# Splitting float64 weights: the high part read before the low word is added, the sum kept in the rounded word's two buffers

## The chip, the core and the metric

The kernel runs on one core of one Trainium2 chip, as one launch. The metric is the device time of an execution in microseconds (us); a run is one such time, and a kernel is told by the median of its runs.

## The reference

Attention over 4 batches, 12 heads, 448 tokens and a head size of 64, with an RMS norm and a gain on queries and keys, and then two mixers over tokens and channels on the result (4 x 448 x 768):

```python
q_n, k_n = rmsnorm(q, g_q), rmsnorm(k, g_k)
x = softmax(q_n @ k_n.T / 8) @ v            # joined heads: 4 x 448 x 768
# mixer 1: rank 32 over tokens, 768 -> 3072 -> 768 over channels
u = x + (xt @ U @ V).transpose(0, 2, 1);     x = u + np.maximum(u @ wa1, 0) @ wa2
# mixer 2: 448 -> 256 -> 448 over tokens, 768 -> 1536 -> 768 over channels
u = x + (np.maximum(xt @ wt1, 0) @ wt2).transpose(0, 2, 1)
x = u + np.maximum(u @ wb1, 0) @ wb2
```

Here xt is x with tokens and channels exchanged. The weights (U, V, wa1, wa2, wt1, wt2, wb1, wb2) arrive as float64, so the kernel reads each as two 32-bit words.

## The kernel before

TensorE multiplies in fp32r. To keep float32 accuracy, most operands are split into a high part (rounded to fp32r) and a low part (what is left of it), and a product is three matmuls: high by high, low by high, high by low (`three`, and the loops in `first` and `second`, line 79 in the profile).

A weight is made from float64 in chunks of up to 128 x 768. For each of them `to_f32` loads the words (L116, tile `w_raw`, two buffers) and then issues: ScalarE takes the absolute value of the high word (L125, into `w_bits`, two buffers); VectorE clamps it (L126), shifts and masks it (L127) and puts sign and top exponent bit back (L131); ScalarE rounds the low word to an integer (L130, into `w_round`, one buffer); GpSimd adds the two (L134, into `w_bits`). `split` then lets ScalarE round the sum to the high part (L144) and GpSimd subtract to get the low part (L145), both into slots `wh` and `wl` of four buffers each, which are free again when TensorE has used a chunk. `load_w` also stores the sum (L159, queue SP, tensors `c_a`, `c_b`) for the chunks that a later stage wants whole, and the split parts (L170, `h_a`, `h_b`). 80 chunks are made in all, 72 of them of 128 x 768.

The work runs in stages. Up to about 195 us there is attention for batches 0 and 1 alone. Then `rank_mix` of these two, and the first channel mixer (`ffn("a", ...)`) for them, with attention for batches 2 and 3 laid between its steps by `run` up to about 610 us; then the rest of that mixer, the token mix, and the second mixer's `ffn("b", ...)`. All weights are made in this part, up to about 940 us. After that `pair_ffn` does the same for batches 2 and 3 with weights from the stores. In `ffn` a group is two chunks of the first weight and two of the second; `first` gives four products per group, and `relu` splits each (ScalarE L628, then VectorE L629, tile `gs`) before `second` can use them.

A scheduler puts the instructions of each engine in order from their dependencies; each engine then works in that order and waits at the first instruction that isn't ready. DMAs are nearly all issued from SP, also in order. VectorE also computes the maxima of the softmax (L445), the low parts of probabilities (L488, tile `pl`), and the sums onto the residual (L659); ScalarE the exponentials (L447) and copies of transposed probabilities (L484); GpSimd the scaling of the softmax (L450, L454), parts of the norm, and the low part of the mixed activations in the rank and token mix (L556).

## Time and profile before

| | before |
|---|---|
| median of 3 runs | 1542.95 us (1540.15 to 1544.28) |
| the profiled execution's own time | 1534.37 us |
| its span, first to last instruction | 1532.5 us |
| mean granted TensorE clock | 0.981 |
| TensorE matmul busy | 1440.4 us |
| VectorE, GpSimd, ScalarE busy | 1173.5, 933.7, 744.9 us |

The profiled execution lies 1.87 us above its span and 8.58 us below the median of the runs shown. A busy engine is one whose instruction runs; the granted clock is the share of its full speed that TensorE was given.

### The profile page before, as it was taken

The numbers are of one execution on the slowest core, as the hardware profiler recorded it, in microseconds if no ns is written. First come the engines' busy times: TensorE is split into PE (matmuls) and PEld (weight loads), VectorE is DVE, ScalarE is ACT, GpSimd is POOL, SyncE is SP. The second block draws the span as 40 slices with busy tenths as digits, with TensorE's granted clock in tenths as the row PEclk, the third lists the DMA queues.
The fourth block names the chain that finished last, engine by engine and source line by source line (L and its number), as shares of the span: only waits on it lengthen the run. The fifth ranks groups of instructions, "written<-read, shape, count | busy, mean of one in ns | idle before, by whom it ended". The sixth has DMA issues, their size and how long they took to land.

```text
span 1532.5 us, 22085 instructions
## 1 busy us (share of the span) xinstructions
PE 1440.4 (94%) x7396; PEld 1275.7 (83%) x7396; DVE 1173.5 (77%) x1785; ACT 744.9 (49%) x1507; POOL 933.7 (61%) x963
## 2 busy tenths in 40 slices
PE   4988978899899999999999999999999999999997
PEld 3766667798788989888888998889999998988996
DVE  6888887887778787666876766487989888577876
ACT  4777755666656656343644343235343431334431
POOL 6888977786776666354665444047787755206841
PEclk9999988999999999999999999999999999999999
DMA  6666655767766665664646664364545463423333
GB/s 167 158 154 154 156 179 185 239 208 213 227 184 214 201 212 192 227 217 162 217 146 206 235 238 155 114 235 129 181 129 180 129 186 125 136 84 122 123 122 103
DMA packets 144385, 266.06 MB, mean 174 GB/s; under 512 B 12832, under 2 KB 104448, under 8 KB 144160
## 3 DMA queue, kind: packets, MB, share of 16 engines
q1 hardware_dynamic: 143952, 264.65, 55.5%
q8 instruction: 59, 0.97, 0.3%
q14 instruction: 54, 0.44, 0.1%
q10 hardware_dynamic: 320, 0.00, 0.0%
HBM read 149.72 MB, written 79.10 MB: 149 GB/s over the span
## 4 chain that ended last, share of the span: by engine, by line
PE 65%; DVE 11%; DMA 8%; POOL 7%; ACT 5%; issue 4%; SPq 1%; ACTq 0%; POOLq 0%; DVEq 0%
PE ps_x L79 26%; PE ps_g L79 13%; PE ps_p L79 10%; PE pv L79 3%; PE sc L79 3%; PE pt L473 3%; PE ps_u L79 2%; DVE w_bits L126 2%; PE ps_t L79 2%; DMA ks<-both 1%; POOL w_bits L134 1%; POOL w L145 1%; DMA w_raw<-in_moe_w_ch_dram 1%; ACT p L447 1%; DMA c_a<-w_bits 1%
## 5 line engine op out<-in xcount | busy, mean ns | idle before, releaser
L79 PE MATMUL ps_x<-gs,w 128*128 128x448 f32 x1440 | 327.5, 374 | 16.4 <-DVE gs L629 11.4
L79 PE MATMUL ps_g<-u,w 128*128 128x448 f32 x1440 | 313.3, 370 | 5.8 <-DVE gs L629 2.9
L79 PEld LDWEIGHTS ps_x<-gs,w 128*128 128x128 f32 x1440 | 270.6, 192 | 42.0 <-DVE gs L629 14.1
L79 PEld LDWEIGHTS ps_g<-u,w 128*128 128x128 f32 x1440 | 269.8, 189 | 30.4 <-DVE gs L629 3.2
L79 PE MATMUL ps_x<-gs,w_b 128*128 128x448 f32 x1026 | 226.8, 366 | 5.3 <-DVE xT L821 3.5
L79 PEld LDWEIGHTS ps_x<-gs,w_b 128*128 128x128 f32 x1026 | 191.9, 188 | 22.9 <-DVE xT L821 5.0
L134 POOL TENSOR_TENSOR w_bits<-w_bits,w_round 128x768 uint32<-128x768 uint32 (+3 forms) x80 | 144.7, 1808 | 92.7 <-DVE w_bits L131 43.5
L145 POOL TENSOR_TENSOR w<-w_bits,w 128x768 fp32r<-128x768 f32 (+3 forms) x82 | 149.5, 1829 | 84.2 <-ACT w L144 75.9
L659 DVE TENSOR_TENSOR xT<-ps_x,xT 128x448 f32<-128x448 f32 x216 | 132.2, 617 | 47.3 <-PE ps_x L79 45.5
L145 POOL TENSOR_TENSOR w_b<-w_f,w_b 128x384 fp32r<-128x384 f32 x104 | 118.8, 1158 | 55.4 <-ACT w_b L144 55.3
L454 POOL TENSOR_SCALAR p<-p,sm 112x448 f32<-112x448 f32 x192 | 132.5, 703 | 25.4 <-DVE sm L451 23.3
L447 ACT ACTIVATE p<-sc,nm 112x448 f32<-112x448 f32 x192 | 121.1, 633 | 55.0 <-DVE nm L445 51.1
L295 POOL TENSOR_TENSOR w_f<-w_f 128x384 f32<-128x384 f32 x26 | 37.2, 1432 | 179.5 <-DVE pu L730 69.9
L79 PE MATMUL sc<-ks,qs 128*112 128x448 f32 x384 | 120.5, 406 | 19.0 <-DMA ks<-both 11.3
L445 DVE TENSOR_REDUCE nm<-sc 112x1 f32<-112x448 f32 x192 | 116.1, 614 | 24.2 <-PE sc L79 23.3
L473 PEld LDWEIGHTS pt<-ident,p 112*112 112x112 f32 x768 | 90.1, 135 | 38.8 <-issue 11.2
L473 PE MATMUL pt<-ident,p 112*112 112x112 f32 x768 | 112.4, 262 | 5.7 <-POOL p L454 4.6
L126 DVE TENSOR_SCALAR w_bits<-w_bits 128x768 f32<-128x768 f32 (+3 forms) x80 | 78.0, 975 | 47.9 <-ACT w_bits L125 47.3
L484 ACT ACTIVATE ph<-pt 112x448 fp32r<-112x448 f32 (+1 forms) x168 | 88.7, 543 | 44.7 <-PE pt L473 43.6
L130 ACT ACTIVATE w_round<-w_raw 128x768 uint32<-128x768 uint32 (+3 forms) x80 | 69.7, 871 | 73.6 <-POOL w_bits L134 70.3
L763 ACT ACTIVATE pu<-pu 128x448 f32<-128x448 f32 x56 | 32.4, 579 | 136.2 <-DVE pu L752 136.1
L125 ACT ACTIVATE w_bits<-w_raw 128x768 f32<-128x768 f32 (+3 forms) x80 | 69.9, 875 | 56.4 <-POOL w L145 36.2
(139 smaller groups left out, 2780.0 us busy)
## 6 DMA issues: line engine op xcount, KB each, us to landing
w_raw<-in_moe_w_ch_dram SPq DMA_DIRECT2D x72, 768.0 KB, 5.1
w_b<-h_a SPq DMA_DIRECT2D x65, 384.0 KB, 4.2
h_a<-w SPq DMA_DIRECT2D x56, 384.0 KB, 3.0
ks<-both SPq DMA_DIRECT2D x92, 224.0 KB, 3.6
c_a<-w_bits SPq DMA_DIRECT2D x40, 384.0 KB, 5.1
w_f<-c_a SPq DMA_DIRECT2D x40, 384.0 KB, 3.2
h_b<-w SPq DMA_DIRECT2D x32, 384.0 KB, 2.7
w_b<-h_b SPq DMA_DIRECT2D x29, 384.0 KB, 4.1
```

The costliest lines, as they stand in the source:

```text
L79: nc.tensor.matmul(o, lhsT=l, rhs=r, start=start, stop=stop)
L125: nc.scalar.activation(f(w), f(high), AF.Abs)
L126: nc.vector.tensor_scalar_max(f(w), f(w), TINY)
L130: nc.scalar.activation(r, low, AF.Copy, scale=2.0 ** -29)
L134: nc.gpsimd.tensor_tensor(w, w, r, op=ALU.add)
L145: nc.gpsimd.tensor_sub(lo, w, f(hi))
L445: nc.vector.tensor_reduce(nm, sc, axis=AX.X, op=ALU.max, negate=True)
L447: nc.scalar.activation(p, sc, AF.Exp, bias=nm, accum_out=sm[:, c % 2:c % 2 + 1])
L454: nc.gpsimd.tensor_scalar(x, x, sm[:, i:i + 1], 1.0, op0=ALU.mult, op1=ALU.mult)
L473: nc.tensor.transpose(pt[:, c * CP:(c + 1) * CP], pr[c][:, kc * CP:(kc + 1) * CP], ident[:CP, :CP],)
L484: nc.scalar.activation(ph, pt, AF.Copy)
L659: nc.vector.tensor_add(xT[:, dc], px, xT[:, dc])
```

## The change

`to_f32` now returns two values. The first, `near`, is `w_bits` after VectorE's last step: it holds sign, exponent and the upper 20 bits of the mantissa. The second is the sum, which GpSimd now writes over the rounded word `w_round`. `split` rounds the high part from `near`, so this instruction depends on VectorE alone, and the low part is still the sum less the high part. The rounded word has two buffers, one in the old place and one in a pool `cv` (chunks take them in turn). The pool takes the place of the unused pool `hs` in the first stages and is opened again with the buffers of the second mixer. `pl` has two buffers instead of three from the end of the first attention on. The store L159 reads the sum from `w_round`. No instruction is added or dropped.

```diff
--- before.py
+++ after.py
@@ -110,6 +110,8 @@
         return pool.tile(shape, F32, tag=pool.name, name=name)
 
 
+    turns = [0]
+
     def to_f32(srcs, p, n):
         raw = wp.tile([P, n], I64, tag="raw", bufs=2, name="w_raw")
         for o, d in srcs(raw):
@@ -119,7 +121,9 @@
         words = raw[:p].bitcast(U32).rearrange("p (n t) -> p n t", t=2)
         low, high = words[:, :, 0], words[:, :, 1]
         w = wp.tile([P, n], U32, tag="w", bufs=2, name="w_bits")[:p]
-        r = wp.tile([P, n], U32, tag="r", name="w_round")[:p]
+        pool, tag = (wp, "r") if turns[0] % 2 else (pools["cv"], "r2")
+        turns[0] += 1
+        r = pool.tile([P, n], U32, tag=tag, bufs=1, name="w_round")[:p]
 
 
         nc.scalar.activation(f(w), f(high), AF.Abs)
@@ -131,8 +135,8 @@
         nc.vector.scalar_tensor_tensor(
             w, high, 0xC0000000, w, op0=ALU.bitwise_and, op1=ALU.bitwise_or
         )
-        nc.gpsimd.tensor_tensor(w, w, r, op=ALU.add)
-        return f(w)
+        nc.gpsimd.tensor_tensor(r, w, r, op=ALU.add)
+        return f(w), f(r)
 
     def slots(key=None, n=DM):
 
@@ -140,8 +144,8 @@
             return [wp.tile([P, n], F32R, tag=t, bufs=4, name="w") for t in ("wh", "wl")]
         return [pools["wt"].tile([P, n], F32R, tag=key + t, name="w") for t in ("h", "l")]
 
-    def split(w, hi, lo):
-        nc.scalar.activation(hi, w, AF.Copy)
+    def split(w, hi, lo, near=None):
+        nc.scalar.activation(hi, w if near is None else near, AF.Copy)
         nc.gpsimd.tensor_sub(lo, w, f(hi))
 
     cache, parts = {}, {}
@@ -153,16 +157,16 @@
             if len(src.shape) == 3:
                 t = t.rearrange("p (a b) -> p a b", a=src.shape[1])
             return [(t, src)]
-        w = to_f32(srcs, p, n)
+        near, w = to_f32(srcs, p, n)
         if cols_:
             cache[keep] = dram.tile([p, n], F32, name=f"c_{keep}")
             nc.sync.dma_start(cache[keep], w)
         hi, lo = slots(key, n if key else DM)
         hi, lo = hi[:p, :n], lo[:p, :n]
         if view is None:
-            split(w, hi, lo)
+            split(w, hi, lo, near)
         else:
-            split(view(w), cols(hi), cols(lo))
+            split(view(w), cols(hi), cols(lo), view(near))
         if keep:
             parts[keep] = dram.tile([p, 2, n], F32, name=f"h_{keep}")
             for i, t in enumerate((hi, lo)):
@@ -171,7 +175,7 @@
         return hi, lo
 
     def load_uv(keep):
-        w = to_f32(
+        near, w = to_f32(
             lambda raw: [(raw[:CP].rearrange("p (c r) -> p c r", c=NC4),
                           U.rearrange("(p c) r -> p c r", c=NC4))], CP, NC4 * R)
         if keep:
@@ -181,11 +185,11 @@
             u4 = slots()[0]
             vh, vl = slots()
         u4 = u4[:CP, :NC4 * 4 * R].rearrange("p (c t r) -> p c t r", c=NC4, t=4)
-        w = w.rearrange("p (c r) -> p c r", c=NC4)
+        near, w = [t.rearrange("p (c r) -> p c r", c=NC4) for t in (near, w)]
         for t in (0, 2):
-            split(w, u4[:, :, t], u4[:, :, t + 1])
-        w = to_f32(lambda raw: [(raw[i * R:(i + 1) * R], V) for i in range(4)], P, S)
-        split(toks(w), cols(vh[:, :S]), cols(vl[:, :S]))
+            split(w, u4[:, :, t], u4[:, :, t + 1], near)
+        near, w = to_f32(lambda raw: [(raw[i * R:(i + 1) * R], V) for i in range(4)], P, S)
+        split(toks(w), cols(vh[:, :S]), cols(vl[:, :S]), toks(near))
         return u4, vh[:, :S], vl[:, :S]
 
     def load_wt():
@@ -1023,7 +1027,7 @@
 
     wt, wtd, kept = [], [], []
     with ExitStack() as stack:
-        open_pools(stack, (("hs", 1, 0), ("at", 2, 0)))
+        open_pools(stack, (("cv", 1, 0), ("at", 2, 0)))
         inner = stack.enter_context(ExitStack())
         AT.update(p=12, ph=4, pl=4)
         open_pools(inner, (("pp", 1, 0), ("s", 3, 1), ("t", 1, 1), ("p", 4, 1)))
@@ -1050,7 +1054,7 @@
         w1s = [w1_chunk("a", wa1, j) for j in range(G)]
         pools["late"] = False
         inner.close()
-        AT.update(p=8, ph=3, pl=3)
+        AT.update(p=8, ph=3, pl=2)
         open_pools(stack, (("pp", 1, 0), ("g", 2 * G + 1, 0), ("p", 2, 1), ("v", 1, 1),
                            ("s", 2, 1), ("t", 1, 1), ("m", 2, 1)))
         pools["new_xs"] = lambda: pools["g"].tile([P, 2, S], F32R, tag="g", name="xs")
@@ -1068,7 +1072,7 @@
             open_pools(rest, (("x3", 1, 0), ("g", 7, 0)))
             open_pools(rest_banks, (("p", 2, 1),))
             plain_banks()
-            open_pools(first_pair, (("xs", 6, 0), ("uv", 1, 0), ("wt", 1, 0)))
+            open_pools(first_pair, (("xs", 6, 0), ("uv", 1, 0), ("wt", 1, 0), ("cv", 1, 0)))
             pools["new_xs"] = lambda: pools["xs"].tile([P, 2, HALF], F32R, tag="xs", name="xs")
             wt.extend(load_wt())
             kept.extend(load_uv(True))
```

The change also alters the order in which the scheduler puts instructions. After the diff, lines below 113 stand 2 to 4 lines further down: L125 of before is L129, L130 is L134, L134 is L138, L144 is L148, L628 is L632, L450 and L454 are L454 and L458.

On ScalarE, in the first mixer with attention beside it, this stands around the last `relu` of a group (`gs_4991`); `w_bits_5487` and `w_round_5488` belong to one chunk, `w_round_5507` to the next, and `both` and `p` to attention. Before:

```order
L125 ACTIVATE w_bits_5487<-w_raw_5485 128x768
L130 ACTIVATE w_round_5488<-w_raw_5485 128x768
L628 ACTIVATE gs_4969<-ps_g_4950 128x448
L411 ACTIVATE both_5858<-tt_5853,gg_78 128x448
L130 ACTIVATE w_round_5507<-w_raw_5504 128x768
L628 ACTIVATE gs_4991<-ps_g_4972 128x448
L144 ACTIVATE w_5246<-w_bits_5236 128x768
```

After the change:

```order
L129 ACTIVATE w_bits_5487<-w_raw_5485 128x768
L451 ACTIVATE p_5343,sm_5337<-sc_5338,nm_5341 112x448
L632 ACTIVATE gs_4969<-ps_g_4950 128x448
L134 ACTIVATE w_round_5488<-w_raw_5485 128x768
L632 ACTIVATE gs_4991<-ps_g_4972 128x448
L148 ACTIVATE w_5246<-w_bits_5236 128x768
L488 ACTIVATE ph_5352<-pt_5345 112x448
L129 ACTIVATE w_bits_5506<-w_raw_5504 128x768
```

The second chunk's instructions now stand behind `gs_4991`; only the first chunk's rounded word is still ahead of it.

On ScalarE, in the first mixer after attention has ended, this is one group with its four `gs` and four chunks (`w_bits_7787`, `7806`, `8000`, `8019`). Before:

```order
L125 ACTIVATE w_bits_7787<-w_raw_7785 128x768
L628 ACTIVATE gs_7380<-ps_g_7361 128x448
L125 ACTIVATE w_bits_7806<-w_raw_7804 128x768
L628 ACTIVATE gs_7402<-ps_g_7383 128x448
L144 ACTIVATE w_7797<-w_bits_7787 128x768
L130 ACTIVATE w_round_7807<-w_raw_7804 128x768
L628 ACTIVATE gs_7424<-ps_g_7405 128x448
L125 ACTIVATE w_bits_8000<-w_raw_7998 128x768
L130 ACTIVATE w_round_8001<-w_raw_7998 128x768
L628 ACTIVATE gs_7533<-ps_g_7514 128x448
L144 ACTIVATE w_7816<-w_bits_7806 128x768
```

After the change:

```order
L129 ACTIVATE w_bits_7787<-w_raw_7785 128x768
L129 ACTIVATE w_bits_7806<-w_raw_7804 128x768
L134 ACTIVATE w_round_7788<-w_raw_7785 128x768
L632 ACTIVATE gs_7380<-ps_g_7361 128x448
L134 ACTIVATE w_round_7807<-w_raw_7804 128x768
L632 ACTIVATE gs_7402<-ps_g_7383 128x448
L148 ACTIVATE w_7797<-w_bits_7787 128x768
L129 ACTIVATE w_bits_8000<-w_raw_7998 128x768
L134 ACTIVATE w_round_8001<-w_raw_7998 128x768
L632 ACTIVATE gs_7424<-ps_g_7405 128x448
L632 ACTIVATE gs_7533<-ps_g_7514 128x448
```

The first two words are read one after the other, and the third and the fourth `gs` stand behind the third chunk's rounded word, where before only the fourth did.

On GpSimd, at the seam where the rank mix ends and attention starts again, `sm` and `p` belong to the softmax of the first head and `w_bits_3744` and `w_bits_3763` to two chunks. Before:

```order
L450 TENSOR_SCALAR sm_3246<-sm_3246 112x2
L134 TENSOR_TENSOR w_bits_3744<-w_bits_3744,w_round_3745 128x768
L450 TENSOR_SCALAR sm_3265<-sm_3265 112x2
L454 TENSOR_SCALAR p_3252<-p_3252,sm_3246 112x448
L454 TENSOR_SCALAR p_3259<-p_3259,sm_3246 112x448
L134 TENSOR_TENSOR w_bits_3763<-w_bits_3763,w_round_3764 128x768
```

After the change:

```order
L138 TENSOR_TENSOR w_round_3745<-w_bits_3744,w_round_3745 128x768
L454 TENSOR_SCALAR sm_3246<-sm_3246 112x2
L138 TENSOR_TENSOR w_round_3764<-w_bits_3763,w_round_3764 128x768
L454 TENSOR_SCALAR sm_3265<-sm_3265 112x2
L458 TENSOR_SCALAR p_3252<-p_3252,sm_3246 112x448
```

Both additions have moved ahead of the first head's scaling.

## Rows read from the trace of the kernel before

**Rows 1.** The page, busy time, share of the span and instructions

```profile
PE 1440.4 (94%) x7396; PEld 1275.7 (83%) x7396; DVE 1173.5 (77%) x1785; ACT 744.9 (49%) x1507; POOL 933.7 (61%) x963
```

**Rows 2.** Windows: busy per engine (instructions), granted clock, DMA share, GB/s

```profile
200.00:240.00 40.00, 35.10 (x149) 28.05 (x149) 31.35 (x45) 24.66 (x46) 31.17 (x26) 0.81 0.51 179
...
1120.00:1160.00 40.00, 40.00 (x199) 37.07 (x198) 35.06 (x41) 14.24 (x29) 29.84 (x28) 1.00 0.59 182
...
410.00:420.00 10.00, 6.88 (x33) 6.17 (x34) 7.40 (x15) 7.76 (x16) 4.29 (x4) 0.83 0.72 249
```

**Rows 3.** Waits of TensorE's matmuls: us in total, times, longest

```profile
PE ps_x L79 <- DVE gs L629: 11.4, 5, 3.3
...
PE ps_x L79 <- POOL w L145: 1.0, 1, 1.0
```

**Rows 4.** Waits inside the making of weights, same columns

```profile
POOL w L145 <- ACT w L144: 75.9, 29, 11.8
...
ACT w_round L130 <- POOL w_bits L134: 70.3, 35, 5.3
...
ACT w L144 <- POOL w_bits L134: 32.0, 22, 4.2
...
ACT w_bits L125 <- DMA c_a<-w_bits: 9.3, 4, 3.4
```

**Rows 5.** Groups by line and form: busy us, mean ns, idle before, releasers

```profile
L134 POOL TENSOR_TENSOR w_bits<-w_bits,w_round 128x768 uint32<-128x768 uint32 x72 | 136.6, 1897 | 88.2 <-DVE w_bits L131 39.1 <-issue 23.8 <-PE ps_x L79 6.4
...
L126 DVE TENSOR_SCALAR w_bits<-w_bits 128x768 f32<-128x768 f32 x72 | 71.6, 995 | 44.6 <-ACT w_bits L125 44.1
```

**Rows 6.** Timeline at 411 us, ScalarE, VectorE, TensorE: start, us, [idle before]

```profile
411.08 0.89 ACT L130 ACTIVATE w_round<-w_raw 128x768 uint32<-128x768 uint32 x1 [3.32 <-DMA w_raw<-in_moe_w_ch_dram]
...
412.44 0.63 DVE L629 SCALAR_TENSOR_TENSOR gs<-ps_g,gs 128x448 fp32r<-128x448 f32 x1 [3.96 <-ACT gs L628]
...
413.12 4.12 PE L79 MATMUL ps_x<-gs,w 128*128 128x448 f32 x12 [3.33 <-DVE gs L629]
```

**Rows 7.** Timeline at 302 to 307 us, ScalarE, VectorE, TensorE

```profile
302.52 0.89 ACT L125 ACTIVATE w_bits<-w_raw 128x768 f32<-128x768 f32 x1 [2.01 <-DMA c_a<-w_bits]
...
304.11 0.54 ACT L628 ACTIVATE gs<-ps_g 128x448 fp32r<-128x448 f32 x1
...
306.05 0.62 DVE L629 SCALAR_TENSOR_TENSOR gs<-ps_g,gs 128x448 fp32r<-128x448 f32 x1
...
306.71 2.38 PE L79 MATMUL ps_x<-gs,w 128*128 128x448 f32 x6 [2.88 <-DVE gs L629]
```

**Rows 8.** Timeline at 635 to 639 us, ScalarE and TensorE

```profile
634.78 0.89 ACT L125 ACTIVATE w_bits<-w_raw 128x768 f32<-128x768 f32 x1 [2.58 <-DMA c_a<-w_bits]
...
638.44 3.88 PE L79 MATMUL ps_x<-gs,w 128*128 128x448 f32 x18 [1.96 <-DVE gs L629]
```

**Rows 9.** Timeline at 544 to 548 us, VectorE and TensorE

```profile
544.28 3.05 DVE L131 SCALAR_TENSOR_TENSOR w_bits<-w_raw,w_bits 128x768 uint32<-128x768 uint32 x1
...
547.92 4.40 PE L79 MATMUL ps_g<-u,w 128*128 128x448 f32 x14 [2.88 <-DVE gs L629]
```

**Rows 10.** Timeline of the rank mix (ScalarE) and token mix (TensorE)

```profile
201.32 0.84 ACT L144 ACTIVATE w<-w_bits 128x768 fp32r<-128x768 f32 x1 [3.06 <-POOL w_bits L134]
...
228.91 0.91 ACT L130 ACTIVATE w_round<-w_raw 128x768 uint32<-128x768 uint32 x1 [2.70 <-POOL w_bits L134]
...
748.09 0.47 PE L79 MATMUL ps_u<-w,xs 128*128 128x448 f32 x1 [1.40 <-ACT xs L608]
```

**Rows 11.** Timeline at 210 and 237 us (VectorE), 238 (GpSimd), 244 (TensorE)

```profile
210.62 0.62 DVE L126 TENSOR_SCALAR w_bits<-w_bits 128x768 f32<-128x768 f32 x1 [0.65 <-ACT w_bits L125]
...
237.44 5.10 DVE L126 TENSOR_SCALAR w_bits<-w_bits 128x768 f32<-128x768 f32 x1
...
238.11 1.84 POOL L145 TENSOR_TENSOR w<-w_bits,w 128x768 fp32r<-128x768 f32 x1
...
243.88 1.09 PE L79 MATMUL sc<-ks,qs 128*112 128x448 f32 x2 [3.87 <-ACT p L447]
```

## The prediction

> **What bounds the kernel now.** I read the page first. TensorE's matmuls are busy for 1440.4 of 1532.5 us, 94% [rows 1], so all that any change of order can win is the 92 us in which TensorE stands still, and the time in which it runs at a lower granted clock. The windows say where that is. While weights come from the stores, TensorE is busy all of 40 us at clock 1.00 (199 matmuls, so 0.201 us each); in the rank mix it is busy for 35.10 of 40 us at a mean clock of 0.81; and after a single stall at 410 us the mean clock of those 10 us is 0.83 [rows 2]. A stall therefore costs its length and something behind it. Of the clock's two levels, 1.2 and 2.4 GHz, a mean of 0.83 is a stretch partly at the lower one, here after TensorE had stood for about 3 us.
>
> Then the list of TensorE's waits: for the low part of a weight it waits once, 1.0 us. For `gs`, the low part of an activation, it waits 11.4 us in five pieces [rows 3]. So the weights are on time; what the making of weights costs is the place that its instructions hold in the queues of ScalarE and VectorE, ahead of work that TensorE does wait for. Those queues do stand still for it: GpSimd waits 75.9 us for ScalarE's high part before its subtraction, ScalarE 70.3 us for GpSimd's addition before it may write the single rounded word, 32.0 us for the sum before the high part, and 9.3 us for the store `c_a` to have read a word buffer [rows 4]. The change goes at all four. The question is how much of these 188 us, on engines that are 49% to 61% busy, is in front of something urgent.
>
> **The change part by part.** No instruction comes or goes, so the busy times should stay; 72 additions of 1897 ns remain 72 additions [rows 5]. What moves is priced at the five places where the timeline shows a stall of TensorE behind the making of weights. The profiled execution took 1534.37 us, 1.87 above its span; the median of the runs shown is 8.58 us higher, and I carry the difference over to it.
>
> *The stall at 413 us*, 3.33 us. ScalarE stood 3.32 us at the rounded word L130 of a second chunk, whose load landed at 411.08; the last `gs` of the group was queued behind it, VectorE idled 3.96 us for it, and TensorE 3.33 [rows 6]. In the new order that L130 stands behind the `gs`. Only the first chunk's L130 is ahead, whose load had landed. I take all 3.3 us, and the 1.7 us that ten microseconds at 0.83 lack against 1.00 [rows 2]. Bounds 0 (the first chunk's word now waits for a store) and 5.0.
>
> *The stalls at 307 and 638 us*, 2.88 and 1.96 us. ScalarE waited at L125 for the store `c_a` (2.01 and 2.58 us), and `gs` was behind it [rows 7, 8]. This wait is not removed. The store now reads the rounded word's buffer, so it is L130 of the same chunk that must wait for it, and the order shows `gs` behind that L130. What goes is what VectorE had to do after L125: its three steps for the chunk came ahead of its half of `gs`, which started at 306.05 though ScalarE's half was done at 304.65 [rows 7]. With L125 free to go early, VectorE is idle by then. I take 1.0 us at each, with bounds of 0 and the whole stalls.
>
> *The stall at 548 us*, 2.88 us: VectorE reached `gs` late because the second chunk's three steps came ahead of it, the last of them 3.05 us long [rows 9]. In the new order this chunk's L125 follows the first chunk's at once and no longer an exponential that had to wait for a maximum, so its steps come sooner, but still ahead of `gs`. I take half, 1.4 us, between 0 and 2.9.
>
> *The rank mix and the token mix.* In the rank mix ScalarE stands 3.06 us for a sum before a high part and 2.70 us for an addition before a rounded word, with copies for TensorE queued behind [rows 10]; both waits are of the removed kinds. TensorE is idle for 4.9 us of the 40 [rows 2]; I take 2.5, between 0 and 4.9, as VectorE's own queue holds the rest. In the token mix TensorE waits 1.40 us for a ScalarE copy behind such instructions [rows 10]: 0.7, between 0 and 1.4.
>
> The gains add up to 3.3 + 1.7 + 1.0 + 1.0 + 1.4 + 2.5 + 0.7 = 11.6 us; their upper bounds to 5.0 + 2.9 + 2.0 + 2.9 + 4.9 + 1.4 = 19.1.
>
> *Two buffers for `pl`.* VectorE may write a low part of probabilities only when TensorE has used the last but one. In the changed order there are nine places in the second attention where that product stands behind the transposes the new part is made from, by 46 matmuls in all: at 0.201 us each [rows 2] at most 9.2 us of waiting on VectorE, and nothing if ScalarE's copy, which precedes each `pl`, takes as long. I take 2 us, nearer to nothing, since the largest gap is 12 matmuls (2.4 us).
>
> *Additions that come earlier.* At the seam both additions now stand ahead of the first head's scaling on GpSimd. Behind them wait the transposes on TensorE. Two additions are 3.8 us [rows 5]; some of it is the time in which GpSimd waited for the exponentials anyway. I take 1.5, between 0 and 3.8.
>
> The rest of the edits (where `near` is read, the pool `cv`, the store's new source) costs nothing: the same instructions with other operands. If the cover of early weights were gone, TensorE would feel each late chunk directly; one such wait, 1.0 us, stands in the list today [rows 3].
>
> Sum: 11.6 - 3.5 = 8.1 us. The profiled execution would take 1534.37 - 8.1 = 1526.3, the median 1542.95 - 8.1 = 1534.9, so 1535 us.
>
> **GpSimd and VectorE.** One rule speaks against the change. The same VectorE instruction, L126, took 0.62 us at 210 us and 5.10 us at 237 us; during the long one GpSimd was subtracting, among others, and TensorE then waited 3.87 us [rows 11]. Its mean is 995 ns over 72 [rows 5], so 72 x 0.375 = 27 us of VectorE go this way now. The Trainium skill says in "SBUF — State Buffer", section "Who interferes with whom", that a VectorE instruction in a two-port mode and a GpSimd instruction exclude each other, and that the loser fully blocks until the other has ended; this trace agrees, with the 5.10 us beside the 0.62. By that rule an idle GpSimd is an opening for VectorE, and this change closes openings; it is the third rival below.
>
> **The rivals.** *Nothing that counts moves* (1543 us, 1538.3 to 1547.6). For it: TensorE waits only 1.0 us for weights [rows 3], and at the 307 and 638 us stalls the wait for the store merely changes place. It needs the gain at 413 us to be eaten by a wait elsewhere.
>
> *The `pl` buffers bite.* With the full 9.2 us, half the gains (5.8) and the 1.5 us of the additions, 1543 + 4.9 = 1548 us.
>
> *GpSimd without openings* (slower). The 75.9 us in which GpSimd waited for the high part came in 29 pieces [rows 4]. If a VectorE step loses its opening in one of them, it waits for one more GpSimd instruction, 1.9 us; all 29 are 55 us of VectorE. About half of such waits reached TensorE (27 us on L126 now, against 11.4 + 3.9 us of TensorE's waits behind VectorE) [rows 3, 11]. It decides from 13 pieces on: 13 x 1.9 x 0.5 = 12.4 us turn 1535 into 1547. With 18 pieces it is 17 us, 1552. Against it: the work of GpSimd is the same, and in the new order an addition or subtraction follows directly on another 107 times, before 105 times, so it isn't packed more densely.
>
> **How the numbers follow.** The forecast, 1527 to 1538 us, gets 0.50; a larger gain 0.03; nothing that counts 0.27; the `pl` buffers 0.05; GpSimd without openings 0.15. I call a difference under 0.3%, 4.6 us, no change, which is about what a measurement of this kernel tells apart. So faster 0.53, same 0.27, slower 0.20. The range goes from all upper bounds without a cost, 1543 - 19.1 = 1524, to 1550, short of the last rival's 1552; the likeliest case's own is 1527 to 1538.
>
> **What would show it.** Right: ScalarE's waits for GpSimd at the rounded word and the high part (102 us) shrink to under 40; GpSimd's wait for the high part falls from 75.9 to under 25; L125 waits for no store, but L130 does; TensorE's waits for `gs` fall from 11.4 to about 6 us; TensorE's busy time stays while its clock at 400 to 420 us rises. Wrong: VectorE waits for TensorE at `pl`; a mean of L126 above 1.2 us; a stall at the seam longer than 3.87 us; or `gs` as late as before because L130 waits longer for the store than L125 did.

## The result, and the profile after

The changed kernel takes 1548.8 us (median of 12 runs, 1539.13 to 1559.15), the kernel before 1540.39 us in the same comparison (12 runs). The ratio is 1.006 with a 95% interval of 1.0036 to 1.0084: slower by about 8 us. The forecast was 1535 us and faster; the range of 1524 to 1550 us holds the result, the sign is wrong. The profiled execution takes 1546.5 us (span 1544.7, mean granted clock 0.978), 12.1 us more than that of before; the medians differ by 8.4, so some 4 us of what the two traces show is particular to these two executions.

The busy line of the page, against [rows 1]:

```profile
PE 1446.0 (94%) x7396; PEld 1275.2 (83%) x7396; DVE 1198.3 (78%) x1785; ACT 743.3 (48%) x1507; POOL 932.2 (60%) x963
```

The same work in the same number of instructions: TensorE has 5.6 us more and VectorE 24.8 us more. The windows, against [rows 2] (busy us and instructions of PE, PEld, DVE, ACT, POOL, then granted clock, DMA share, GB/s):

```profile
200.00:240.00 40.00, 29.55 (x131) 23.89 (x131) 28.07 (x43) 20.86 (x40) 26.27 (x26) 0.84 0.42 144
...
400.00:410.00 10.00, 7.12 (x24) 6.41 (x25) 9.82 (x13) 3.29 (x7) 8.43 (x9) 0.66 0.96 325
...
410.00:420.00 10.00, 10.00 (x56) 9.09 (x56) 6.50 (x13) 5.90 (x11) 6.91 (x5) 1.00 0.81 245
```

The 410 to 420 us window, 6.88 us busy at 0.83 before [rows 2], is now full at 1.00; the one ahead of it, which [rows 2] doesn't show, fell from 8.94 us at 1.00 to 7.12 at 0.66. And the 40 us with most of the rank mix have lost 5.55 us of TensorE's work: 29.55 where it was 35.10 [rows 2].

TensorE's waits after the change, against [rows 3] (us in total, times, longest):

```profile
PE ps_x L79 <- DVE xT L663: 8.0, 7, 2.3
...
PE ps_u L79 <- DVE xs L582: 7.0, 5, 2.8
...
PE ps_h L79 <- ACT xs L553: 6.6, 3, 4.8
...
PE ps_x L79 <- DVE gs L633: 5.7, 7, 2.2
...
PE ps_g L79 <- DVE gs L633: 4.3, 2, 4.1
...
PE ps_u L79 <- DVE xs L613: 4.1, 1, 4.1
...
PE pv L79 <- DVE pl L492: 2.8, 7, 0.6
```

Rows of the same list of before that were not shown:

```profile
PE ps_h L79 <- ACT xs L549: 3.7, 3, 2.7
...
PE ps_u L79 <- DVE xs L578: 2.6, 3, 1.2
...
PE ps_u L79 <- DVE xs L609: 1.5, 2, 1.1
...
PE ps_x L79 <- DVE xT L659: 1.5, 3, 0.7
...
PE pv L79 <- DVE pl L488: 0.6, 3, 0.3
```

The wait for `gs` that the change was priced by has halved, from 11.4 to 5.7 us [rows 3]; that of the first products for `gs` (`ps_g`) is 4.3 us and was 2.9, the one stall of [rows 9]. What has grown stands in other rows: the sums on the residual that TensorE's bank waits for (`xT`, 1.5 to 8.0), and the copies of `rank_mix` and `token_mix` on VectorE and ScalarE (`xs`: L582 2.6 to 7.0, L553 3.7 to 6.6, L613 1.5 to 4.1).

Waits inside the making of weights, against [rows 4]:

```profile
POOL w L149 <- ACT w L148: 80.1, 20, 12.2
...
ACT w L148 <- PE ps_x L79: 58.0, 7, 10.6
...
ACT w_bits L129 <- DMA w_raw<-in_moe_w_ch_dram: 40.7, 25, 4.1
...
ACT w_round L134 <- POOL w L149: 35.5, 26, 2.4
...
ACT w_round L134 <- DMA c_a<-w_round: 5.8, 3, 2.7
```

ScalarE waits for GpSimd 35.5 us, where it was 70.3 + 32.0 us [rows 4]. But GpSimd waits for the high part as long as before, 80.1 us against 75.9, and ScalarE's first step has a wait that was 0.9 us before: 40.7 us for the load of the raw words. By form, against [rows 5]:

```profile
L130 DVE TENSOR_SCALAR w_bits<-w_bits 128x768 f32<-128x768 f32 x72 | 78.8, 1095 | 48.2 <-ACT w_bits L129 47.5 <-POOL w_round L138 0.4
```

GpSimd's addition (L138) is as long as ever, 1901 ns where it was 1897; VectorE's three steps of the 72 large chunks (L130, L131, L135) have grown from 218.2 us to 246.7 together.

**Where the time is.** I cut each span at the transposes of the rank mix (tile `pt_x`) and at the first products of the token mix (`ps_t`). The view of a tile shows count, shortest, median and longest ns, and first and last start. Before:

```profile
L543 PE MATMUL pt_x<-ident,xT x48: 270/273/421, 182.9 to 230.1; 128*112 128x128 f32 x48
...
L79 PE MATMUL ps_t<-xs,w x96: 333/338/426, 735.5 to 792.2; 112*128 112x384 f32 x96
```

After:

```profile
L547 PE MATMUL pt_x<-ident,xT x48: 270/273/421, 182.3 to 235.7; 128*112 128x128 f32 x48
...
L79 PE MATMUL ps_t<-xs,w x96: 333/338/525, 741.3 to 800.6; 112*128 112x384 f32 x96
```

| us | before | after | difference |
|---|---|---|---|
| up to the first `pt_x` | 182.9 | 182.3 | -0.6 |
| rank mix, first to last `pt_x` | 47.2 | 53.4 | +6.2 |
| to the first `ps_t` | 505.4 | 505.6 | +0.2 |
| token mix, first to last `ps_t` | 56.7 | 59.3 | +2.6 |
| to the end | 740.3 | 744.1 | +3.8 |

The two mixes, 7% of the span, carry 8.8 of the 12.2 us. The long stage between them, in which the stalls at 307, 413, 548 and 638 us and the seam lie, came out level: what went there came back elsewhere in it. The 3.8 us at the end aren't waits. TensorE is busy 721.5 us there, where it was 717.2, and the granted clock of the stretch from 1212 to 1412 us is 0.98 and 0.97, where it was 1.00. This end also differs between kernels of one order: with `pl` at two in the order of before (below), which is no slower than before, it is 745.2 us long.

The start of the rank mix after the change, from the timeline (start, us, [idle before <- what ended it]); ScalarE, TensorE, VectorE, TensorE:

```profile
195.97 0.89 ACT L129 ACTIVATE w_bits<-w_raw 128x768 f32<-128x768 f32 x1 [2.58 <-DMA w_raw<-in_moe_w_ch_dram]
...
198.86 0.87 ACT L553 ACTIVATE xs<-pt_x 112x384 fp32r<-112x384 f32 x2
...
199.41 0.69 PE L79 MATMUL ps_h<-xs,w 112*128 112x384 f32 x1 [4.83 <-ACT xs L553]
...
216.10 1.40 DVE L131 TENSOR_SCALAR w_bits<-w_bits 128x768 uint32<-128x768 uint32 x1
...
217.53 2.45 DVE L135 SCALAR_TENSOR_TENSOR w_bits<-w_raw,w_bits 128x768 uint32<-128x768 uint32 x1
...
220.00 0.56 DVE L582 TENSOR_TENSOR xs<-ps_h,xs 64x384 fp32r<-64x384 f32 x1
...
220.62 1.86 PE L79 MATMUL ps_u<-w,xs 128*128 128x448 f32 x4 [2.82 <-DVE xs L582]
```

ScalarE stands 2.58 us at a raw word that hasn't landed, with the first copies (L553) queued behind, and TensorE stands 4.83 us for these. At 216 us VectorE does two weight steps, 1.40 and 2.45 us long, ahead of the copy L582, and TensorE stands 2.82 us. The same places before the change:

```profile
194.60 0.89 ACT L125 ACTIVATE w_bits<-w_raw 128x768 f32<-128x768 f32 x1 [0.52 <-DMA w_raw<-in_moe_w_ch_dram]
...
197.40 0.87 ACT L549 ACTIVATE xs<-pt_x 112x384 fp32r<-112x384 f32 x2
...
197.94 0.69 PE L79 MATMUL ps_h<-xs,w 112*128 112x384 f32 x1 [2.67 <-ACT xs L549]
...
213.14 1.49 DVE L126 TENSOR_SCALAR w_bits<-w_bits 128x768 f32<-128x768 f32 x1
...
214.66 0.56 DVE L578 TENSOR_TENSOR xs<-ps_h,xs 64x384 fp32r<-64x384 f32 x1
...
215.26 1.47 DVE L127 TENSOR_SCALAR w_bits<-w_bits 128x768 uint32<-128x768 uint32 x1
```

There ScalarE stood 0.52 us at that word and TensorE 2.67 us; and on VectorE the copy (L578) stood between the first step and the second of the chunk. Nothing in the edit touches these copies. On VectorE the copy has another place in the queue. On ScalarE it has not: but for one step of 0.21 us (L376) the same instructions stand between the word and the first copies. What differs there is when the load lands. SP issued it at the same time, before and after:

```profile
189.68 0.47 SPq L116 DMA_DIRECT2D w_raw<-in_moe_w_ch_dram  x1
...
189.64 0.45 SPq L118 DMA_DIRECT2D w_raw<-in_moe_w_ch_dram  x1
```

From its issue to the step that reads it 4.9 us pass before and 6.3 after. Why it is longer isn't shown.

Outside the rank mix, the new stall at 402.88 us and the one in the token mix:

```profile
402.88 6.08 PE L79 MATMUL ps_g<-u,w 128*128 128x448 f32 x18 [4.09 <-DVE gs L633]
...
772.60 2.45 DVE L135 SCALAR_TENSOR_TENSOR w_bits<-w_raw,w_bits 128x768 uint32<-128x768 uint32 x1
...
774.98 1.01 DVE L613 SCALAR_TENSOR_TENSOR xs<-ps_t,xs 128x384 fp32r<-128x384 f32 x2
...
775.58 0.93 PE L79 MATMUL ps_u<-w,xs 128*128 128x448 f32 x3 [4.11 <-DVE xs L613]
```

At 402.88 us TensorE waits for `gs` as it did at 413 us, here behind a weight step of 3.43 us on VectorE; in the token mix the step L135, 2.45 us, stands ahead of L613, and TensorE waits 4.11 us.

### The profile page after: what moved, and what is told of

It reads as the page before. It is cut to its first block, busy times and chain, and to the rows that moved or that the text cites. A ratio compares the mean times of both kernels' runs of the same rounds, so it can differ in the third digit from the quotient of the medians.

```text
span 1544.7 us, 22120 instructions
## 1 busy us (share of the span) xinstructions
PE 1446.0 (94%) x7396; PEld 1275.2 (83%) x7396; DVE 1198.3 (78%) x1785; ACT 743.3 (48%) x1507; POOL 932.2 (60%) x963
## 4 chain that ended last, share of the span: by engine, by line
PE 53%; DVE 12%; DMA 6%; issue 4%; ACT 3%; POOL 2%; SPq 1%; ACTq 0%; DVEq 0%; POOLq 0%
PE ps_x L79 24%; PE ps_g L79 10%; PE ps_p L79 10%; DMA w_raw<-in_moe_w_ch_dram 3%; DVE w_bits L130 3%; DVE w_bits L135 2%; PE ps_u L79 2%; PE ps_t L79 2%; DVE w_bits L131 1%; ACT w_bits L129 1%; PE pv L79 1%; DMA qs<-both 1%; PE sc L79 1%; DMA c_a<-w_round 1%; PE pt_x L547 1%
## 5 line engine op out<-in xcount | busy, mean ns | idle before, releaser
L138 POOL TENSOR_TENSOR w_round<-w_bits,w_round 128x768 uint32<-128x768 uint32 (+3 forms) x80 | 145.4, 1817 | 106.0 <-DVE w_bits L135 70.3
L149 POOL TENSOR_TENSOR w<-w_round,w 128x768 fp32r<-128x768 f32 (+3 forms) x82 | 148.7, 1821 | 83.3 <-ACT w L148 80.1
L149 POOL TENSOR_TENSOR w_b<-w_f,w_b 128x384 fp32r<-128x384 f32 x104 | 118.0, 1148 | 59.1 <-ACT w_b L148 58.9
L458 POOL TENSOR_SCALAR p<-p,sm 112x448 f32<-112x448 f32 x192 | 130.8, 693 | 20.6 <-DVE sm L455 17.1
L130 DVE TENSOR_SCALAR w_bits<-w_bits 128x768 f32<-128x768 f32 (+3 forms) x80 | 84.2, 1053 | 50.6 <-ACT w_bits L129 49.9
L148 ACT ACTIVATE w<-w_bits 128x768 fp32r<-128x768 f32 (+3 forms) x82 | 65.5, 818 | 86.3 <-PE ps_x L79 58.0
L135 DVE SCALAR_TENSOR_TENSOR w_bits<-w_raw,w_bits 128x768 uint32<-128x768 uint32 (+3 forms) x80 | 96.0, 1200 | 0.9
```

The lines of the kernel that those rows point to most:

```text
L130: nc.vector.tensor_scalar_max(f(w), f(w), TINY)
L135: nc.vector.scalar_tensor_tensor(w, high, 0xC0000000, w, op0=ALU.bitwise_and, op1=ALU.bitwise_or)
L138: nc.gpsimd.tensor_tensor(r, w, r, op=ALU.add)
L148: nc.scalar.activation(hi, w if near is None else near, AF.Copy)
L149: nc.gpsimd.tensor_sub(lo, w, f(hi))
L458: nc.gpsimd.tensor_scalar(x, x, sm[:, i:i + 1], 1.0, op0=ALU.mult, op1=ALU.mult)
```

## Experiments

"Held order" in the edits below is a function at the kernel's end that ties every instruction of an engine to the one ahead of it in a list, without a wait, so that the scheduler's choice is fixed. Neither kernel ran in its own list with nothing else changed; the nearest is `pl` at two in the list of before (the last of these runs), 0.9986 of the kernel before. Where the function stands, the diff is this, and the text says whose list it is:

```diff
+        for a, b in zip(ranks, ranks[1:]):
+            tc.add_manual_dep(traced[e][b], traced[e][a].name, my.DependencyInfo(
+                my.DependencyClass.NoSync, my.DependencyReason.DATA), reason="in_order")
```

**The parts alone.** Two rounded words without the early high part:

```diff
-        nc.scalar.activation(hi, w if near is None else near, AF.Copy)
+        nc.scalar.activation(hi, w, AF.Copy)
```

> The changed kernel with one part undone: the high part is again made from the sum, so GpSimd again waits for ScalarE between the addition and the subtraction; the two buffers, the sum in the rounded word and two buffers of pl stay. GpSimd without openings: VectorE's three weight steps (218 us in 72 chunks before, 247 us after) fall back to 215 to 228 us, GpSimd again waits some 60 to 80 us in the openings, and the time is back within 3 us of before's (about 1540). The pl buffers, or the two buffers as such: it stays as slow as the changed kernel, 1546 to 1551, with VectorE's steps short. Only the order drawn by the scheduler: any time from 1535 to 1550, without relation to the sum of the weight steps.

1579.0 us, 1.0244 (1.0218 to 1.027). ScalarE's wait for raw words, in the list of waits:

```profile
ACT w_bits L129 <- DMA w_raw<-in_moe_w_ch_dram: 141.3, 61, 6.0
```

The early high part without the second buffer (sum still in the rounded word, `pl` at three):

```diff
-        pool, tag = (wp, "r") if turns[0] % 2 else (pools["cv"], "r2")
-        r = pool.tile([P, n], U32, tag=tag, bufs=1, name="w_round")[:p]
+        r = wp.tile([P, n], U32, tag="r", name="w_round")[:p]
```

> The kernel before with the other part alone: the high part from the upper 20 bits, the sum in the rounded word, which has one buffer; three buffers of pl. GpSimd without openings: VectorE's weight steps stay above 235 us and the time is 1545 to 1552, since the high part does not wait for the addition. If the second buffer is what costs (bursts of two chunks, raw loads late): steps at 218 us and 1538 to 1542. pl: 1538 to 1542 as well, since pl has its three buffers. ScalarE must wait longer for the single rounded word than the 70.3 us of before, since it is now held until the subtraction has read it.

1589.6 us, 1.0312 (1.029 to 1.0334). `pl` alone, on the kernel before:

```diff
-        AT.update(p=8, ph=3, pl=3)
+        AT.update(p=8, ph=3, pl=2)
```

> The kernel before with two buffers of pl and nothing else. The pl buffers as the cause: 1545 to 1549, with VectorE waiting for TensorE at pl and TensorE waiting several us for pl. The other theories: within 2 us of before.

1531.28 us, 0.993 (0.9907 to 0.9952), faster than both kernels. The parts come to +38, +48 and -10 us, the whole to +8. None of the three lies in a range that was expected, and they don't add up; a part whose only effect can be a wait (a buffer less) made the kernel faster. So I take it that each of the three also carries a new order from the scheduler, and that a part cannot be priced this way. For `pl` a run below shows it; for the other two it is argued.

**What VectorE and GpSimd cost each other.** A kernel of its own, on data of no meaning: each VectorE instruction eight times alone, then sixteen times beside eight of GpSimd's additions, as here:

```python
for _ in range(N):
    nc.gpsimd.tensor_tensor(g, g, h, op=ALU.add)
for _ in range(2 * N):
    nc.vector.tensor_scalar_max(f(d), f(d), TINY)
```

> Not the reference's work: the three weight steps of VectorE (clamp, shift, merge), an addition from PSUM and one within SBUF, each 8 times alone and then 16 times beside 8 additions of GpSimd over 768 columns, and the clamp beside 8 subtractions. GpSimd without openings: a weight step beside GpSimd takes its own 0.55 to 0.94 us alone, but beside GpSimd it waits for whole GpSimd instructions, so the mean of those that run beside it is above 1.5 us, while the additions from PSUM stay at 0.61 us. If instead the steps are only slowed in proportion (shared bandwidth), all of them lengthen by the same 20 to 60% and none to more than 1.5 us.

The view of a line (ns shortest/median/longest), the clamp alone and beside, the merge (the form of the third weight step) alone and beside, a sum from PSUM alone and beside, then GpSimd's addition alone and beside the merge:

```profile
L99 DVE TENSOR_SCALAR d<-d x8: 547/548/548, 2.9 to 9.9; 128x768 f32<-128x768 f32 x8
...
L123 DVE TENSOR_SCALAR d<-d x16: 559/1298/2040, 63.0 to 83.7; 128x768 f32<-128x768 f32 x16
...
L105 DVE SCALAR_TENSOR_TENSOR d<-w_raw,d x8: 957/958/959, 15.6 to 22.6; 128x768 uint32<-128x768 uint32 x8
...
L135 DVE SCALAR_TENSOR_TENSOR d<-w_raw,d x16: 957/1698/2441, 107.3 to 134.0; 128x768 uint32<-128x768 uint32 x16
...
L108 DVE TENSOR_TENSOR e<-ps,e x8: 610/616/616, 3.4 to 10.4; 128x448 f32<-128x448 f32 x8
...
L141 DVE TENSOR_TENSOR e<-ps,e x16: 624/624/624, 135.9 to 145.8; 128x448 f32<-128x448 f32 x16
...
L115 POOL TENSOR_TENSOR g<-g,h x8: 1797/1798/1799, 32.2 to 45.4; 128x768 uint32<-128x768 uint32 x8
...
L133 POOL TENSOR_TENSOR g<-g,h x8: 2393/2397/2435, 107.4 to 124.8; 128x768 uint32<-128x768 uint32 x8
```

Only half of the sixteen have an addition beside them, so the medians mix two lengths. In order of time, the first clamp starts ahead of the additions and takes 559 ns; the next eight, one for each addition, take 2037 to 2040 ns; the last seven, behind the last addition, 559 to 560. With the merge, eight take 2437 to 2441 ns and eight 957 to 959. So each step beside GpSimd waits for one GpSimd instruction. GpSimd is lengthened too, 1798 to 2397 ns beside the merge. The instruction with one operand in PSUM keeps 624 ns. So the third rival's mechanism is real. Whether it makes the difference is another question.

**The additions taken away.** Both kernels in their own held order, with the addition over one of the columns:

```diff
-        nc.gpsimd.tensor_tensor(r, w, r, op=ALU.add)
+        nc.gpsimd.tensor_tensor(r[:, :1], w[:, :1], r[:, :1], op=ALU.add)
```

> The changed kernel with every instruction of all five engines queued in the changed kernel's own order, and GpSimd's 72 additions (and those of U, V and the token weights) done over one column in place of 768: the other columns of a weight are not summed. So only the length of these GpSimd instructions differs from the changed kernel. GpSimd's hold on VectorE: the three weight steps fall from 247 us to 180 to 205, TensorE's stalls behind VectorE in the rank mix and the token mix shorten, and the time falls by 10 us or more, to 1530 to 1540. Order of the instructions alone, or late raw loads: the same stalls remain and the time stays within 4 us of the changed kernel's 1549.

> The kernel before in its own order, with the same additions over one column. Its waits for the addition (102 us of ScalarE's) go too. GpSimd's hold: steps from 218 us to 165 to 185, time 1525 to 1533, and the distance between the changed kernel and the kernel before shrinks from 8 us to under 4. Order alone: the distance stays at 6 to 10 us.

1531.38 us (0.9946, 0.9928 to 0.9963) and 1523.49 us (0.9899, 0.9875 to 0.9923). Both gain 16 to 18 us, and the gap stays at 7.9. The weight steps are 202.2 and 187.4 us: their gap shrank from 28.5 to 14.8 us, that of the time hardly did (from 8.4). The changed kernel alone, at 1531, would have spoken for GpSimd's hold; the kernel before, treated alike, speaks against it.

**The same GpSimd work in halves**, in held order, so that a blocked step waits for less:

```diff
+        op(*[x[:, :n] for x in (o, a, b)])
+        followers.add(op(*[x[:, n:] for x in (o, a, b)]).ins.name)
```

> The changed kernel in its own order, all work done, but each addition and each subtraction of a weight on GpSimd in two instructions of half the columns, one behind the other. GpSimd's hold: a step of VectorE has an opening between the halves, so a blocked step waits for one half, about 1 us, and not for 1.9; the steps fall by 25 to 50 us and the time by 5 to 12 us, to 1537 to 1544. Order alone: no faster than 1546, and slower by what the 144 more instructions cost GpSimd if that is late anywhere.

> The kernel before in its own order with the same halves. GpSimd's hold: steps from 218 us to 180 to 200, TensorE's stall of 3.87 us at 244 us (behind the 5.10 us clamp) shorter, time 1530 to 1537. Order alone: 1539 to 1543.

1548.48 us (1.0052, 1.0035 to 1.0069) and 1547.9 us (1.0048, 1.003 to 1.0067). The steps shortened by 17.6 us in the changed kernel (to 229.1) and by 17.1 in the one before (to 201.1). The first gained nothing, the second lost 0.5%. The halves also keep GpSimd busy longer, by 44.9 us in the first (320.7 for 275.8, additions and subtractions) and 26.8 in the second, so neither run prices the steps by itself. But the two kernels are only 0.6 us apart here, while their steps still differ by 28.0 us: the length of VectorE's steps doesn't set the difference by itself.

**Weight steps moved by hand.** The changed kernel in its own held order, with ten groups of weight steps put behind the copies that TensorE waited for; on VectorE for instance:

```
 L130 TENSOR_SCALAR w_bits<-w_bits 128x768
-L131 TENSOR_SCALAR w_bits<-w_bits 128x768
-L135 SCALAR_TENSOR_TENSOR w_bits<-w_raw,w_bits 128x768
 L582 TENSOR_TENSOR xs<-ps_h,xs 64x384
 L554 TENSOR_TENSOR xs<-pt_x,xs 112x384 x2
+L131 TENSOR_SCALAR w_bits<-w_bits 128x768
+L135 SCALAR_TENSOR_TENSOR w_bits<-w_raw,w_bits 128x768
```

> The changed kernel in its own order but for ten groups of ScalarE's and VectorE's weight steps (L129, L134, L148; L130, L131, L135), each moved behind the one or two copies for TensorE that stood behind it: in the rank mix (stalls of 4.83, 2.55 and 2.82 us), at 250, 277, 403 and 731 us (1.81, 2.30, 4.09, 2.27) and in the token mix (4.11). All work is done, nothing else moves. If the place of these steps in the two queues is the loss: these stalls, 24.8 us, shrink to under 12, and the time falls by 6 to 14 us, to 1535 to 1543. If the time is lost elsewhere, or a later weight takes it back: 1546 or more.

> The kernel before with two buffers of pl (1531 us), in its own order but for seven groups of weight steps moved in the same way, at 200 to 205 us (stalls of 2.79 and 1.65), 248 (4.38, behind a clamp of 4.89), 310 (1.32) and 743 (1.55 and 1.15). If the place in the queue is what costs: 1520 to 1528. If not: 1530 to 1533.

1553.87 us (1.0064, 1.0044 to 1.0084), no gain; the kernel with `pl` at two, treated alike, 1531.1 us (0.9935, 0.9911 to 0.996), as without the move. In the first, the wait for L582 went from 7.0 to 3.8 us and another copy became late; in the list of TensorE's waits:

```profile
PE ps_u L79 <- DVE xs L582: 3.8, 4, 1.5
...
PE ps_h L79 <- DVE xs L554: 7.9, 3, 5.0
```

The second of them was 3.0 us without the move. That a few steps at a few places are the whole of it has fallen.

**The rounded word held too long.** Was the loss that of a word that stays taken until the subtraction? Two buffers with the sum back in `w_bits`; and the early high part with the addition behind it, also into `w_bits`:

```diff
-        nc.gpsimd.tensor_tensor(r, w, r, op=ALU.add)
+        nc.gpsimd.tensor_tensor(w, w, r, op=ALU.add)
```

> The kernel before with two buffers of the rounded word and two of pl; the sum stays in the first word and the high part is made from it. So a rounded word is free after the addition, not after the subtraction and the store. If holding the rounded word until the subtraction is what keeps the raw buffer and makes the loads late (141 and 119 us of ScalarE's waits for raw words in the two parts alone): these waits fall under 30 us and the time is 1526 to 1541. If two rounded words as such are bad: 1550 or more, as with the first part alone.

> The kernel before with two buffers of pl and the high part from the upper 20 bits, ahead of the addition, which stays in the first word and waits for the high part; one rounded word, free after the addition; the store of the word stands behind the split in the text. If holding the rounded word is the cause: ScalarE's waits for raw words under 30 us, time 1526 to 1541. If the early high part as such is bad: 1550 or more, as with the second part alone.

1584.65 us (1.0266, 1.0231 to 1.03) and 1595.62 us (1.0343, 1.0317 to 1.0369): neither recovers anything. ScalarE waits for raw words 134.1 us in the first (at L134), and only 13.5 in the second, where the early high part alone had 118.9; the second is no faster for it. Both kernels also drew an order of their own, so this speaks against the idea and doesn't exclude it.

**The loads.** Held orders; of each chunk 128 of 768 columns are loaded and read six times over, so that the words land early:

```diff
+                o, d = o[:, :k], d[:, :k]
...
+            low, high = [t[:, :P].unsqueeze(1).to_broadcast([P, n // P, P]) for t in (low, high)]
```

> The changed kernel in its own order; of each chunk's raw words only the first 128 of 768 columns are loaded, and ScalarE's and VectorE's steps read them six times over (so the weights are not the reference's); every instruction and its size otherwise as before. Late loads as the cause: ScalarE's 41 us of waits for raw words fall under 8, and the time falls by 6 us or more, to 1543 or less, more than the control falls. If the order or the steps' length is the cause: the time falls no more than the control does.

> The same cut of the loads in the kernel before, in its own order: the control. ScalarE waits for raw words for 4 us there, so late loads would give 0 to 3 us; a larger fall would be what less traffic gives to the other transfers (stores of words, 16 us of ScalarE's waits; keys and queries, 11 us of TensorE's).

> The same cut in the first part alone (two rounded words, sum in the rounded word, high part from the sum; 1579 us), in that kernel's own order. Late loads as the cause: its 141 us of waits for raw words fall under 25 and the time falls by 20 us or more, to 1559 or less. If not: 1570 or more.

The changed kernel 1538.17 us (0.9971, 0.9954 to 0.9988), the one before 1529.58 (0.9916, 0.9888 to 0.9944): ScalarE's wait for raw words falls from 40.7 to 3.3 us in the first, and TensorE's for the copy L553 from 6.6 to 2.6. Yet both kernels gain about 13 us (0.9% and 0.8% of their ratios), and 8.6 us stay between them. Two buffers alone go from 1579.0 to 1546.88 us (1.004, 1.0017 to 1.0063), 32 us; less the 13 that the other kernels gain too, about half of that part's 38 us was late loads by this count. The rest of it I did not find.

**The order by itself.** The changed kernel with the rank mix (177 to 237 us) and the token mix (722 to 805) of every engine in the order of the kernel before; the kernel before with its rank mix and the start of the next stage (179 to 254 us) in the order of the changed one; and `pl` at two with the whole order of the kernel before. Of the second, VectorE:

```
+L126 TENSOR_SCALAR w_bits<-w_bits 128x768
+L127 TENSOR_SCALAR w_bits<-w_bits 128x768
+L131 SCALAR_TENSOR_TENSOR w_bits<-w_raw,w_bits 128x768
+L578 TENSOR_TENSOR xs<-ps_h,xs 64x384
...
-L126 TENSOR_SCALAR w_bits<-w_bits 128x768
 L578 TENSOR_TENSOR xs<-ps_h,xs 64x384
-L127 TENSOR_SCALAR w_bits<-w_bits 128x768
```

> The changed kernel, all work done, in its own order on all engines except in the rank mix (177 to 237 us) and the token mix (722 to 805 us): there each engine's instructions stand as in the kernel before (274 rows of TensorE's, 80 of VectorE's, 71 of ScalarE's, 36 of GpSimd's and 34 of SP's change place). If the drawn order in these two stages is the loss: the rank mix falls from 61.5 to 56 to 58 us, the token mix from 59.2 to 56 to 58, and the time by 5 to 9 us, to 1540 to 1544. If the change's own dependences are (the rounded word held until the subtraction, weights that come at other times): the stages stay above 60 and 59 us and the time at 1547 or more.

> The kernel before in its own order, except in the rank mix and the start of the next stage (179 to 254 us), where each engine's instructions stand as in the changed kernel. If the drawn order is the loss: the rank mix rises from 55.6 to 59 to 62 us and the time by 3 to 6 us, to 1544 to 1547. If the change's dependences are: within 2 us of the kernel before.

> Two buffers of pl in the order of the kernel before, on all engines. If the 10 us that two buffers of pl alone gained are those of a better order: 1539 to 1545, that is the kernel before or a little slower, with a few us of VectorE's waits for TensorE at pl. If the buffers themselves (other addresses, other waits) gain: 1529 to 1535.

| | median us | ratio to before | its interval |
|---|---|---|---|
| changed, mixes in the order of before | 1546.37 | 1.0029 | 1.0014 to 1.0044 |
| before, rank mix in the changed order | 1548.92 | 1.0049 | 1.0031 to 1.0066 |
| `pl` at two in the order of before | 1539.58 | 0.9986 | 0.9972 to 1.0 |

The transposes of the rank mix run from 183.7 to 233.1 us in the first. In the second, with three of TensorE's and ScalarE's stalls:

```profile
L543 PE MATMUL pt_x<-ident,xT x48: 270/272/421, 183.4 to 238.2; 128*112 128x128 f32 x48
...
197.95 0.89 ACT L125 ACTIVATE w_bits<-w_raw 128x768 f32<-128x768 f32 x1 [3.58 <-DMA w_raw<-in_moe_w_ch_dram]
...
201.39 0.69 PE L79 MATMUL ps_h<-xs,w 112*128 112x384 f32 x1 [5.84 <-ACT xs L549]
...
222.85 0.74 PE L79 MATMUL ps_g<-u,w 128*128 128x448 f32 x1 [3.31 <-ACT w L144]
```

The kernel before, not one instruction of it changed, loses 0.49% when the rank mix and the start of the next stage take the other's order, and its weight steps are 218.1 us, as short as ever. It shows the first stall again (ScalarE 3.58 us at the raw word, which landed 7.6 us after its issue; TensorE 5.84). The second it does not: where the changed kernel waits 2.82 us for the copy L582, this one waits 3.31 us for a high part, behind a ScalarE that stands 3.87 us for GpSimd to free the single rounded word. That is a wait of the kind that the change removes. So an order alone can cost this much, but 0.49% is not what it costs the changed kernel. Put back, the order of before shortens the rank mix of the changed kernel by 4.0 us (49.4 for 53.4), while its token mix got 2.7 us longer (62.0); in all about half of the loss is gone, though the intervals of 1.0029 and 1.006 overlap, and 1546.37 lies between what was expected of the order and of the dependences. And the 0.7% that `pl` at two seemed to win was the order it drew: held in an order of its own, it keeps it (0.9935, above), and in the order of before it doesn't (0.9986).

**The mixes in seven pairs.** First to last `pt_x` plus first to last `ps_t`, from the view of the tiles, and the difference of the medians:

| pair | rank mix us | token mix us | both together | medians |
|---|---|---|---|---|
| changed, before | 53.4, 47.2 | 59.3, 56.7 | +8.8 | +8.4 |
| the same without additions | 49.4, 45.0 | 59.9, 53.1 | +11.2 | +7.9 |
| the same with early loads | 51.7, 46.6 | 59.0, 56.0 | +8.1 | +8.6 |
| the same in halves | 52.6, 49.0 | 57.2, 58.9 | +1.9 | +0.6 |
| before with the changed rank mix, before | 54.8, 47.2 | 57.9, 56.7 | +8.8 | +7.5 |
| changed with the mixes as before, before | 49.4, 47.2 | 62.0, 56.7 | +7.5 | +4.5 |
| changed with steps moved by hand, before | 54.8, 47.2 | 62.4, 56.7 | +13.3 | +9.9 |

For the last three rows the difference is the ratio less 1, times 1540 us. With the additions there or gone, with loads early or late, the gap in time goes with that in the two mixes, within 3.4 us of it; where the mixes came out nearly alike, so did the time. These are pairs whose orders come from the two kernels. Where the scheduler drew another order for the whole, it doesn't hold: against before, `pl` at two with steps moved has mixes 3.8 us longer and is 10.0 us faster, and the two parts alone that cost 38 and 48 us have mixes only 10.2 and 4.8 us longer. Each length is of one profiled execution.

## Why the prediction was wrong, step by step

**The bound** was read rightly: TensorE, 94% busy, and its waits on VectorE's and ScalarE's queues.

**The waits inside the making of weights** did as forecast in part. Those for GpSimd fell to 35.5 us (under 40 was said), L129 no longer waits for the store and L134 does, for 5.8 us. GpSimd's wait for the high part did not fall, 80.1 us where under 25 was said: the high part is no longer held up by the sum, but L148 now waits 58.0 us (28.7 before) for TensorE to give its slot back.

**The stall at 413 us** went, but one of 4.09 us at 402.88 us took its place, and the granted clock of 400 to 420 us fell, where I had said that it would rise: (0.66 + 1.00) / 2 = 0.83 from (1.00 + 0.83) / 2 = 0.92. **Those at 307 and 638 us** went whole: 2.88 + 1.96 = 4.8 us, where I took 2.0. **The one at 548 us** went, and the nearest wait for `gs` is one of 0.96 us at 556.62: 1.9 gained for 1.4. **At the seam** the additions ahead of the softmax cost nothing: 3.87 us before, 0.62 and 1.81 now; I had charged 1.5. **`pl`**, charged 2: TensorE waits 2.8 us for it where it was 0.6, and in the order of before the buffer costs nothing (0.9986). With these, the stage between the mixes should have gained 8.4 - 3.5 = 4.9 us by my terms; it came out at +0.2: among what it lost, `xT` is waited for 6.5 us more, all of the 8.0 us between 249 and 731 us. Each price was near; the sum left out what the new order puts in front of other consumers.

**The rank mix and the token mix** are the step that failed most. I took 2.5 + 0.7 us of gain, on the ground that waits of the removed kinds stood ahead of TensorE's copies there. These waits did go. But TensorE waits longer there for others: 4.83 us for copies behind a raw word that landed late, 2.82 and 4.11 us for copies that the scheduler's new order puts behind two and three weight steps in a row; and the stages became 6.2 + 2.6 us longer. The two wrong numbers are 3.2 + 8.8 = 12.0 us of the 20.3 between a forecast of -8.1 and the 12.2 of the spans; the stage between is 5.1, start and end the other 3.2. That an order of the rank mix can cost so much is shown on the kernel before (0.49%, in part by another wait); in the changed kernel the old order gave 4.0 us of the rank mix back. Late loads don't explain that stage: with early ones it is still 5.1 us longer than that of before. For the token mix the order isn't shown to be the cause, since the old order made it longer. I had compared the two orders at `gs` and at the seam, and not in these stages.

**The rivals.** *Nothing that counts moves* is out by the interval. *The `pl` buffers bite* gave the right time, 1548, for a wrong reason; that is luck, as it is that the range, whose upper end was set by another rival, holds the result. *GpSimd without openings* had the right sign, and its 28.5 us of VectorE are there (against 55 at most); its price of half of that, 14 us, is not: with the additions gone or halved the steps shorten and the gap doesn't follow them. None of the signs that I listed for it, or for any loss, came: L130 has a mean of 1.095 us, below 1.2, the seam is shorter, TensorE waits less for `gs`, and VectorE waits for nothing of TensorE's at `pl`.

**Open.** The 4 to 5 us that the changed kernel with its mixes in the old order still loses; its token mix was 62.0 us long, and whether longer steps or the joints of the two orders make that wasn't separated. Also open is why the load ahead of the first copies lands later, and why two of the parts alone cost 38 and 48 us, beyond the late loads in the first.

## What to carry to other kernels

When a scheduler orders the queues, an edit has two effects, the waits it takes away and the order that it redraws, and the second can be larger and far from the edit: compare old and new order in every stage where engines hand short copies to the engine that sets the time, not only where the removed wait was. To price an edit, or a part of one, hold the order, and look whether a borrowed order makes waits that its own kernel didn't have, as the 3.31 us above. Without a held order, `pl` at two looked like -0.7% and was nothing, and parts of +38, +48 and -10 us made a whole of +8.

## What was not expected of the hardware

A VectorE step with its operands in SBUF and a GpSimd addition alternate, one for one: each clamp that had an addition beside it took 2037 to 2040 ns, where it took 548 alone, each such merge 2437 to 2441, where it took 958, and GpSimd's additions 2397 ns beside the merge, where they took 1798, while a VectorE sum with one operand in PSUM stayed at 624. The Trainium skill says in "SBUF — State Buffer", section "Who interferes with whom", that a VectorE instruction with two SBUF inputs contends with GpSimd's reads, and one with at most one of them only in the two-port modes, which it gives to forms like the clamp; the merge, the clamp and the sum from PSUM agree. Halving the GpSimd instructions takes 17 us from VectorE's steps and gives no time: in the changed kernel two halves take 2 x 1132 ns where one addition took 1901. And taking the additions away is worth 16 to 18 us to either kernel, though TensorE waits for GpSimd's low parts only once, for 1.0 us [rows 3].
